# Routing a batch in parts and loading a later batch's input behind other transfers, in a Fourier mixing and mixture-of-experts kernel

## The chip, the cores and the metric

The kernel runs on one core of a Trainium2 chip. The core has a matrix engine (TensorE, PE in the profile, its weight loads PEld), a vector engine (VectorE, DVE), a scalar engine (ScalarE, ACT), GpSimd (POOL) and a queue engine (SyncE, SP), and 16 DMA engines that move data between the main memory and the on-chip memory. Each engine runs its own instructions in the order in which they were recorded, and waits on semaphores for the others. The metric is the time of one execution on the device, in microseconds (us).

## The reference

Two blocks follow each other. The first takes x of 8 batches, 2496 positions and 256 channels, and keeps the real part of a Fourier transform over both axes:

```python
X = np.fft.fft(x, axis=1)
X = np.fft.fft(X, axis=2)
return X.real.astype(np.float32)
```

The second treats the 19968 rows of the result as tokens of a mixture of 8 experts in which no token is dropped. Each token goes to the expert with the largest logit, through a hidden layer of 1024, and its result is scaled by that expert's probability:

```python
logits = x @ w_gate
expert_idx = np.argmax(logits, axis=1)
...
    h = np.maximum(x_sorted[lo:hi] @ w1[e], 0.0)
    y_sorted[lo:hi] = h @ w2[e]
return (gate_w[:, None] * y).astype(np.float32)
```

## The kernel before

The transform over 2496 positions is split as 104 times 24, and works batch by batch.

The first stage (`first`, line 325) reads x in three tiles per batch. `load` (284) issues one such transfer of 896 KB on SyncE's queue into one of three buffers `xq`. `fold` (299) adds and subtracts mirrored halves on VectorE, in two steps; `half1` (311) multiplies by the table of waves on TensorE (results `s1`), ScalarE copies them to `t1`, and a transfer writes them to a scratch tensor `Td` in main memory. `regroup` (351) reads `Td` back in another order as two tiles `t4`.

The second stage (`second`, 361) works in groups of 120 columns. `group` makes `p2` on TensorE, which ScalarE copies to `zz`; `turn_last` (365) is a small rotation `pr` of a column. Ten pairs of 128-row slices follow, five to each half: two products make `p3`, ScalarE copies part of it to `zs` (405), VectorE copies the logits to `lg` (408) and writes two slices of `rows` (410), and `mirror` (383), on ScalarE, fills the mirrored columns of the pair before.

`route` (416) then handles the five pairs of a half, ten slices, at once. VectorE finds the largest logit and its expert, one-hot in `oh`; TensorE counts the tokens ahead of each one with ten small products into `rk`; VectorE turns the counts into places `pi` in a buffer `Xs` in main memory that is sorted by expert. Each slice of `rows` is one scatter by index on GpSimd's queue (`send`, 462, through `put_row`, 235). A batch has 20 of them. For batches after 0, ScalarE and GpSimd first copy the index (468, 469).

`plan` (478) computes on one partition of VectorE which expert each block of rows belongs to. All its tables are 21 (`MOST`) columns wide, whatever the number of blocks. `experts` (729) works through the blocks: it fetches a block's rows `xb` (526) and the expert's weights (542) on SyncE's queue, transposes the rows (`turn`, 577: VectorE at 583, ScalarE at 586), and multiplies by the two weight matrices (`ph`, then `py`); another scatter on GpSimd writes the output. Batch 0 gives two blocks of 256 and four of 128 rows, batch 1 four of 256, the later ones blocks of 512.

The order of the work is that in which the Python program records it. Stages are generators, and each `yield` is a place at which other work can be woven in. Before any expert block: the first stage of batch 0; seven steps of `ahead_of(1)` (first stage and regrouping of batch 1); then `second(0)` with one more step of it at every second yield and a `send` at each. From line 996 on, `experts` drives the record: for every piece of expert work it does, side steps fall due (`next(side)`), and these are the plans, the next batches' stages and the sends. `mixed(b)` (935) weaves the second stage of batch b with the first stage of b + 1. The first block is recorded so, in lines 777 to 786:

```python
while todo[0][:3] not in tabs:
    yield 0, False
fetch_some(0, 1)
while b not in whole:
    yield 0, True
fetch_some(0)
for _ in range(9):
    yield 0, False
for xT in turn(b, size, xbs[0][0]):
    pass
```

Here each `yield 0, False` makes one side step, `fetch_some(0, n)` issues the row and weight fetches of the first n blocks, and `whole` holds a batch once all its scatters are recorded. Batch 2's three x tiles are loaded from within the first stage of batch 1 (line 344).

Of the kernel before, what the change touches and what calls it, by code (L numbers as in the profile page):

```python
# [12 lines left out]
F32 = mybir.dt.float32  # L13
BF16 = mybir.dt.bfloat16
# [167 lines left out]

TICKS = 32
LATE = 4
SHARE, EARLY, ROOM = 0.6, 0.7, 1.2
AHEAD = 12
WARM = 16
# [28 lines left out]
def kernel(ctx: ExitStack, tc, x, w_gate, w1, w2, out):  # L216
# [108 lines left out]
    def first(b):  # L325

        pm0 = xp.tile([NA, D], F32, tag="pm0", name="pm0")
        for q in range(NQ + 1):
            f = iter(())
            if q < NQ:  # L330
                xq = ahead.pop((b, q))
                f = fold(xq, q, pm0[:])
            next(f, None)
            yield
            if q:
                t1 = xp.tile([NP, 4, D], F32, tag="t1", name="t1")
                half1(b, q - 1, 0, pm, pm0, t1)
            next(f, None)
            yield
            if q:  # L340
                half1(b, q - 1, 1, pm, pm0, t1)
                (nc.sync if b > 1 else act).dma_start(out=Td[b][:, 4 * (q - 1) * D:4 * q * D], in_=t1[:].rearrange("p j d -> p (j d)"))
                if b:
                    load(b + 1, q - 1)
            next(f, None)
            pm = xq[:, 4:8]
            yield
# [13 lines left out]
    def second(b):  # L361

        t4 = None

        def turn_last(h):

            nonlocal t4
            t4 = ahead.pop((b, "t4", h))
            n = min(HALF, NG - h * HALF)
            pr = pm_.tile([GP, HALF], F32, tag="m", name="pr")  # L370
            mm(pr[:, 0:n], con["rot"][:], t4[0:GP, 0:n, H])
            act.copy(t4[0:GP, 0:n, H], pr[:, 0:n])

        def group(g):
            i, n = g % HALF, LAST if g == NG - 1 else GP
            p2 = pm_.tile([128, 2, n], F32, tag="m", name="p2")
            for c in range(2):
                mm(p2[:, c], t4[0:GP, i, c * H:(c + 1) * H], con["m2"][:, c, 0:n])
            act.copy(zz[:, :, g * GP:g * GP + n], p2[:])
            if g == HALF - 1:  # L380
                turn_last(1)

        def mirror(rows, k):
            act.copy(free(rows[:], (k + 1) * W + D - 1, [-W, 2], [-1, H - 1]),
                     free(rows[:], k * W + 1, [W, 2], [1, H - 1]))

        turn_last(0)
        yield
        group(0)
        yield  # L390
        group(1)
        yield
        for h in range(2):
            rows = sp.tile([128, NSL, W], F32, tag="rows", name="rows")
            lg = sp.tile([128, NSL, E], F32, tag="lg", name="lg")
            for i in range(HW):
                w, k = HW * h + i, 2 * i
# [18 lines left out]
    def route(b, h, rows, lg):  # L416
# [6 lines left out]
        mx, eq, v = small("mx", NSL), small("eq", NSL, E), small("v", NSL)  # L423
        vec.reduce_max(mx[:], lg[:], axis=AX_X)
        vec.tensor_tensor(eq[:], lg[:], bc(mx[:], 2, E), op=ALU.is_equal)
        vec.tensor_tensor(eq[:], eq[:], bc(con["rev"][:], 1, NSL), op=ALU.mult)
        vec.reduce_max(v[:], eq[:], axis=AX_X)
        vec.tensor_tensor(v[:], v[:], con["good"][:, h], op=ALU.mult)
        oh = small("oh", NSL + 1, E, dt=BF16)
        vec.memset(oh[:, NSL], 0.0)  # L430
        vec.tensor_tensor(oh[:, 0:NSL], bc(con["rev"][:], 1, NSL), bc(v[:], 2, E), op=ALU.is_equal)
        yield

        su = small("su", NSL)
        vec.tensor_tensor(lg[:], lg[:], bc(mx[:], 2, E), op=ALU.subtract)
        act.activation(lg[:], lg[:], ACTF.Exp)
        vec.tensor_scalar(rows[:, :, D], con["row"][:, h], float(b * S), None, op0=ALU.add)
        yield

        rk = pm_.tile([128, NSL + 1, E], F32, tag="m", name="rk")  # L440
        mm(rk[:], tri[:], oh[:], True, False)
        for s in range(NSL):
            mm(rk[:, s + 1:], ones[:], bc(oh[:, s], 1, NSL - s), False, s == NSL - 1)
        vec.reduce_sum(su[:], lg[:], axis=AX_X)
        vec.tensor_scalar(su[:], su[:], 1e-9, None, op0=ALU.add)
        vec.reciprocal(rows[:, :, D + 1], su[:])
        yield

        pos, pf, pi = small("pos", NSL, E), small("pf", NSL), small("pi", NSL, dt=I32)
        vec.tensor_tensor(pos[:], rk[:, 0:NSL], bc(base[:], 1, NSL), op=ALU.add)  # L450
        vec.tensor_tensor(pos[:], pos[:], oh[:, 0:NSL], op=ALU.mult)
        vec.reduce_sum(pf[:], pos[:], axis=AX_X)
        vec.tensor_tensor(pf[:] if b else pi[:], pf[:], con["far"][:, h], op=ALU.add)
        nxt = cp.tile([128, E], F32, tag="base", name="base", bufs=2)
        vec.tensor_tensor(nxt[:], rk[:, NSL], base[:], op=ALU.add)
        base = nxt
        for s in range(NSL):
            waiting.append((b, pf[:, s:s + 1], pi[:, s:s + 1], rows[:, s]))

    waiting = deque()  # L460
# [17 lines left out]
    def plan(b, size, k, last):  # L478
# [3 lines left out]
        def one(name, *dims, dt=F32):  # L482
# [14 lines left out]
        ge, ei = one("ge", MOST, E), one("ei", MOST)  # L497
        val, eq, rw = one("val", MOST, E + 1), one("eq", MOST, E + 1), one("rw", MOST)
        vec.tensor_tensor(ge[:], bc(bk["i"], 2, E), bc(ce[:], 1, MOST), op=ALU.is_ge)
        vec.reduce_sum(ei[:], ge[:], axis=AX_X)  # L500
        yield
        vec.tensor_tensor(eq[:], bc(ei[:], 2, E + 1), bc(bk["e9"], 1, MOST), op=ALU.is_equal)
        vec.memset(val[:, :, E:E + 1], float(E * CAP))
        vec.scalar_tensor_tensor(val[:, :, 0:E], bc(bk["i"], 2, E), float(size), bc(rb[:], 1, MOST),
                                 op0=ALU.mult, op1=ALU.add)
        yield
        vec.tensor_tensor(val[:], val[:], eq[:], op=ALU.mult)
        vec.reduce_sum(rw[:], val[:], axis=AX_X)
        tab = cp.tile([1, 2, MOST], I32, tag="p_tab", name="p_tab", bufs=4)
        vec.tensor_copy(tab[:, 0], rw[:])  # L510
        vec.tensor_scalar(tab[:, 1], ei[:], E - 1.0, None, op0=ALU.min)
# [217 lines left out]
    def experts(todo):  # L729
# [44 lines left out]
        for k, (b, size, last, at) in enumerate(todo):  # L774
            n, m = size // 128, BIG // size
            if not k:
# [303 lines left out]
```

## Time and profile before

| What | us |
|---|---|
| median of three runs | 1263.31 |
| lowest, highest | 1263.24, 1265.31 |
| the profiled execution's own time | 1264.13 |
| its span, from first to last instruction | 1262.3 |
| TensorE busy | 1214.1 |
| VectorE busy | 777.0 |
| ScalarE busy | 424.8 |
| GpSimd busy | 446.1 |

The page of a profile gives for each engine its busy time, its share of the span and its number of instructions; then the span in 40 equal slices, one digit of busy tenths each; then the chain of work that ended last, and the costliest groups by line, operation and tile. TensorE is busy for 96% of the span; its busy time is modelled for pipelined products, so it is read here for where it has gaps and not as a distance from the peak. Questions put to the trace answer for a stretch of time: busy times by stage, the chain of waits, the instructions in order, and how long a transfer took from its issue to its landing.

### The profile page before, as it was taken

What the parts mean: (1) busy time and instruction counts of PE and PEld (TensorE: products, weight loads), DVE (VectorE), ACT (ScalarE), POOL (GpSimd) and SP (SyncE); (2) the same over time, 40 slices, a digit from 0 to 9 for tenths busy, and PEclk for the clock granted to TensorE, in tenths of its full rate; (3) what the DMA queues carried; (4) which work ended last, traced back from release to release, by engine and by line L of the source; (5) the groups of instructions that cost most, each with busy time, mean ns of one, the idle gap of its engine ahead of it and who ended that gap; (6) DMA issues with size and microseconds to landing.
All of it is one profiled execution on the core that took longest, in us unless ns stands there. A gap on an engine that the chain in (4) does not pass through costs nothing.

```text
span 1262.3 us, 22196 instructions
## 1 busy us (share of the span) xinstructions
PE 1214.1 (96%) x7289; PEld 1080.3 (86%) x7289; DVE 777.0 (62%) x1884; ACT 424.8 (34%) x1087; POOL 446.1 (35%) x527
## 2 busy tenths in 40 slices
PE   5769999999999999999999999999999999999997
PEld 3658988777788899888988898889999999999996
DVE  4546334443466788576866578686888784444663
ACT  1423332332243433433344333432333232222222
POOL 0245436154116512472225603472364241111112
PEclk6759999999999999999999999999999999999998
DMA  8869898765348454573336435453346338788887
GB/s 236 272 195 327 304 307 306 204 224 169 126 147 258 138 142 160 154 263 115 101 123 207 141 94 160 140 179 101 105 138 190 109 105 282 284 289 275 285 284 278
DMA packets 163216, 249.79 MB, mean 198 GB/s; under 512 B 118601, under 2 KB 130227, under 8 KB 143516
## 3 DMA queue, kind: packets, MB, share of 16 engines
q1 hardware_dynamic: 146327, 203.28, 51.0%
q0 software_dynamic: 15888, 42.14, 9.3%
q10 hardware_dynamic: 885, 2.94, 0.7%
q8 instruction: 59, 0.97, 0.3%
q14 instruction: 57, 0.47, 0.1%
HBM read 194.91 MB, written 54.83 MB: 198 GB/s over the span
## 4 chain that ended last, share of the span: by engine, by line
PE 62%; issue 17%; DVE 10%; DMA 5%; POOL 4%; ACT 2%; POOLq 0%; SPq 0%; DVEq 0%; ACTq 0%
PE py L221 18%; PE a L221 9%; PE c L221 7%; PE ph L221 6%; PE p L221 6%; PE b L221 5%; PE d L221 4%; PE s L221 3%; PE e L221 3%; POOL out_dram L236 3%; DMA t<-Td 1%; DMA xq<-in_x_dram 1%; POOL Xs L236 1%; DVE xT L583 1%; DMA Td<-t 1%
## 5 line engine op out<-in xcount | busy, mean ns | idle before, releaser
L236 POOL DMA_INDIRECT out_dram<-y,ro x163 | 160.9, 987 | 629.5 <-ACT y L679 299.6
L221 PE MATMUL py<-w_sb,hT 128*128 128x256 f32 x1504 | 340.3, 380 | 0.0
L221 PEld LDWEIGHTS py<-w_sb,hT 128*128 128x128 f32 x1504 | 281.2, 190 | 36.9 <-issue 1.0
L236 POOL DMA_INDIRECT Xs<-rows,pi x160 | 164.2, 1026 | 111.7 <-DVE rows L410 53.0
L221 PE MATMUL ph<-xT,w_sb 128*128 128x128 f32 (+2 forms) x992 | 173.1, 330 | 10.0 <-DVE ro L792 8.8
L221 PEld LDWEIGHTS ph<-xT,w_sb 128*128 128x128 f32 x992 | 137.6, 194 | 34.4 <-issue 16.5
L221 PE MATMUL a<-xT,w_sb 128*128 128x256 f32 (+1 forms) x512 | 117.9, 357 | 0.0
L837 DVE TENSOR_SCALAR hT<-ph 128x512 f32<-128x512 f32 x43 | 29.7, 691 | 127.9 <-PE ph L221 68.2
L586 ACT ACTIVATE xT<-xT 128x256 f32<-128x256 f32 (+1 forms) x94 | 36.5, 388 | 181.7 <-DVE xT L583 137.3
L221 PEld LDWEIGHTS a<-xT,w_sb 128*128 128x128 f32 x512 | 88.5, 190 | 10.0 <-DVE xT L583 0.3
L891 ACT ACTIVATE y<-py,xb 128x256 f32<-128x256 f32 x94 | 44.5, 473 | 153.8 <-PE py L221 152.1
L635 DVE TENSOR_TENSOR hT<-hT,b 128x512 f32<-128x512 f32 x57 | 39.2, 687 | 79.0 <-PE b L221 53.4
L408 DVE COPY lg<-p 128x16 f32<-128x16 f32 x80 | 13.8, 173 | 111.4 <-ACT zs L405 111.3
L645 ACT ACTIVATE hT<-a 128x512 f32<-128x512 f32 x57 | 34.0, 597 | 134.1 <-PE a L221 131.1
L221 PE MATMUL s<-xq,w 104*112 104x256 f32 (+2 forms) x208 | 62.4, 425 | 11.8 <-DVE xq L297 9.5
L469 POOL CAST pi<-due 128x1 int32<-128x1 f32 x140 | 42.2, 302 | 68.4 <-ACT due L468 68.4
L221 PE MATMUL a<-w_sb,hT 128*128 128x128 f32 x528 | 66.0, 276 | 0.0
L221 PEld LDWEIGHTS p<-table,t 120*128 120x128 f32 x352 | 54.7, 206 | 10.6 <-issue 3.1
L221 PEld LDWEIGHTS a<-w_sb,hT 128*128 128x128 f32 x528 | 63.1, 192 | 0.7
L221 PE MATMUL c<-xT,ws 128*128 128x256 f32 (+1 forms) x256 | 60.2, 362 | 1.2 <-DVE hT L641 0.4
L221 PE MATMUL p<-table,zz 128*128 128x145 f32 (+1 forms) x320 | 57.6, 306 | 3.6 <-DVE rows L410 2.4
L583 DVE STREAM_TRANSPOSE xT<-xb 128x512 f32<-128x512 f32 (+1 forms) x91 | 56.3, 631 | 7.0 <-DMA xb<-Xs 7.0
(149 smaller groups left out, 2103.2 us busy)
## 6 DMA issues: line engine op xcount, KB each, us to landing
w_sb<-in_moe_w_dram SPq DMA_DIRECT2D x132, 1024.0 KB, 6.9
xq<-in_x_dram SPq DMA_DIRECT2D x24, 896.0 KB, 8.9
xb<-Xs SPq DMA_DIRECT2D x112, 128.0 KB, 3.3
Td<-t SPq DMA_DIRECT2D x18, 448.0 KB, 3.3
t<-Td SPq DMA_DIRECT2D x8, 768.0 KB, 7.0
t<-Td SPq DMA_DIRECT2D x8, 640.0 KB, 9.3
xb<-Xs SPq DMA_DIRECT2D x52, 64.0 KB, 4.7
xb<-Xs SPq DMA_DIRECT2D x88, 32.0 KB, 4.8
```

The lines of the kernel that those rows point to most:

```text
L221: nc.tensor.matmul(o, lhsT=lhsT, rhs=rhs, start=start, stop=stop, **kw)
L236: return unordered(pool.indirect_dma_start(out=dst, out_offset=bass.IndirectOffsetOnAxis(ap=idx, axis=0), in_=rows, in_offset=None, bounds ...
L408: vec.tensor_copy(lg[:, k:k + 2], p3[:, NY:NY + 2 * E].rearrange("p (m e) -> p m e", m=2))
L469: pool.tensor_copy(idx, due[:])
L583: vec.transpose(free(xT[:], 256 * h, [32, n // 32], [BIG, 2], [1, 32]), free(xb, 512 * h, [64, n // 32], [1, 2], [2, 32]))
L586: act.activation(odd, odd, ACTF.Copy, scale=-1.0)
L635: vec.tensor_tensor(h12, h11, b[:], op=add)
L645: act.activation(h11, a[:], ACTF.Relu)
L837: vec.tensor_scalar(o, ph[:], 0.0, None, op0=ALU.max)
L891: act.activation(y[:, i % 2], py[:], ACTF.Copy, scale=meta[:, i, 1:2])
```

## The change

Six things are changed.

- Batch 0 is routed in four parts, of 2, 3, 3 and 2 pairs (`PARTS`), each with its own counts and scatters. The first two steps of a part's route are recorded at once and the rest after the rows of the next pair.
- VectorE's copy of the logits becomes a ScalarE copy, recorded after the mirror.
- The x tiles of batch 2 are no longer loaded from the first stage of batch 1. The first is loaded after batch 1's regrouping; the second and third are loaded in `experts`, after the fetches of the first two blocks and before the third's.
- Before `second(0)` six steps of batch 1's first stage are recorded and not seven; inside it, one step at each yield from the seventh on, in place of every second.
- In `mixed` the first stage's steps fall on even steps of the second stage in place of odd. Before the first transposition stand 12 side steps in place of 9, and the first five steps of the plans come before the weaving.
- `plan` works on k columns, the number of blocks, in place of `MOST`.

```diff
+PARTS = ((2, 3), (3, 2))
@@ first
-                if b:
+                if b > 1:
                     load(b + 1, q - 1)
@@ second
+            ends = list(np.cumsum(PARTS[h] if not b else (HW,)))
+            lo = 0
...
-                if i:
+                if i and i not in ends:
                     mirror(rows, k - 2)
-                vec.tensor_copy(lg[:, k:k + 2], p3[:, NY:NY + 2 * E].rearrange("p (m e) -> p m e", m=2))
+                act.copy(lg[:, k:k + 2], p3[:, NY:NY + 2 * E].rearrange("p (m e) -> p m e", m=2))
...
+                if pending:
+                    for _ in pending:
+                        pass
+                    pending = None
                 yield
-            mirror(rows, k)
-            yield from route(b, h, rows, lg)
+                if i + 1 in ends:
+                    mirror(rows, k)
+                    pending = route(b, h, rows, lg, slice(lo, k + 2))
+                    if not b and w < NW - 1:
+                        next(pending)
+                        next(pending)
+                    else:
+                        yield from pending
+                        pending = None
+                    lo = k + 2
@@ route: the same operations on n slices, with pf and pi in four buffers
+        n = at.stop - at.start
+        rows, lg = rows[:, at], lg[:, at]
...
@@ plan: the same operations on k columns
-        vec.tensor_tensor(ge[:], bc(bk["i"], 2, E), bc(ce[:], 1, MOST), op=ALU.is_ge)
+        vec.tensor_tensor(ge[:, :, 0:E], bc(count, 2, E), bc(ce[:], 1, k), op=ALU.is_ge)
...
@@ experts
                 while b not in whole:
                     yield 0, True
+                fetch_some(0, 2)
+                load(2, 1)
+                load(2, 2)
                 fetch_some(0)
-                for _ in range(9):
+                for _ in range(12):
                     yield 0, False
@@ ahead_of
         regroup(b, 0)
         regroup(b, 1)
+        if b == 1:
+            load(2, 0)
@@ mixed
-            if k % 2:
+            if k % 2 == 0:
                 next(one, None)
@@ before the expert blocks
-    for _ in range(7):
+    for _ in range(6):
         next(early)
     for k, _ in enumerate(second(0)):
-        if k % 2 == 0:
+        if k >= 6:
             next(early, None)
         send()
...
-            side = woven(chain(close(0), through(0)), chain(early, side))
+            plans = close(0)
+            side = chain(islice(plans, 5), woven(chain(plans, through(0)), chain(early, side)))
```

More of the change, by code (lines that the diff above doesn't have):

```diff
@@ L411, in second, with route @@
                                              op0=ALU.add, op1=op)
+                if pending:
+                    for _ in pending:
+                        pass
+                    pending = None
                 yield
-            mirror(rows, k)
-            yield from route(b, h, rows, lg)
-    def route(b, h, rows, lg):
+                if i + 1 in ends:
[6 more added lines that the diff above has]
+                        yield from pending
+                        pending = None
+                    lo = k + 2
+    def route(b, h, rows, lg, at):
         nonlocal base
@@ L421, in small @@
             return sp.tile([128, *dims], dt, tag=name, name=name)
[L423 to L429, printed above, removed]
@@ L430, in route @@
-        vec.memset(oh[:, NSL], 0.0)
-        vec.tensor_tensor(oh[:, 0:NSL], bc(con["rev"][:], 1, NSL), bc(v[:], 2, E), op=ALU.is_equal)
+        n = at.stop - at.start
+        rows, lg = rows[:, at], lg[:, at]
+        mx, v, su = (small(name, NSL)[:, 0:n] for name in ("mx", "v", "su"))
+        eq, pos = (small(name, NSL, E)[:, 0:n] for name in ("eq", "pos"))
+        pf = sp.tile([128, NSL], F32, tag="pf", name="pf", bufs=4)[:, 0:n]
+        pi = sp.tile([128, NSL], I32, tag="pi", name="pi", bufs=4)[:, 0:n]
@@ L432, in route @@
+        oh = small("oh", NSL + 1, E, dt=BF16)[:, 0:n + 1]
+        vec.reduce_max(mx, lg, axis=AX_X)
+        vec.tensor_tensor(eq, lg, bc(mx, 2, E), op=ALU.is_equal)
+        vec.tensor_tensor(eq, eq, bc(con["rev"][:], 1, n), op=ALU.mult)
+        vec.reduce_max(v, eq, axis=AX_X)
+        vec.tensor_tensor(v, v, con["good"][:, h, at], op=ALU.mult)
+        vec.memset(oh[:, n], 0.0)
+        vec.tensor_tensor(oh[:, 0:n], bc(con["rev"][:], 1, n), bc(v, 2, E), op=ALU.is_equal)
         yield
-        su = small("su", NSL)
@@ L435, in route @@
-        vec.tensor_tensor(lg[:], lg[:], bc(mx[:], 2, E), op=ALU.subtract)
-        act.activation(lg[:], lg[:], ACTF.Exp)
-        vec.tensor_scalar(rows[:, :, D], con["row"][:, h], float(b * S), None, op0=ALU.add)
+        vec.tensor_tensor(lg, lg, bc(mx, 2, E), op=ALU.subtract)
+        act.activation(lg, lg, ACTF.Exp)
+        vec.tensor_scalar(rows[:, :, D], con["row"][:, h, at], float(b * S), None, op0=ALU.add)
         yield
-        rk = pm_.tile([128, NSL + 1, E], F32, tag="m", name="rk")
@@ L441, in route @@
[L441 to L446, printed above, removed]
-        yield
-        pos, pf, pi = small("pos", NSL, E), small("pf", NSL), small("pi", NSL, dt=I32)
-        vec.tensor_tensor(pos[:], rk[:, 0:NSL], bc(base[:], 1, NSL), op=ALU.add)
@@ L451, in route @@
-        vec.tensor_tensor(pos[:], pos[:], oh[:, 0:NSL], op=ALU.mult)
-        vec.reduce_sum(pf[:], pos[:], axis=AX_X)
-        vec.tensor_tensor(pf[:] if b else pi[:], pf[:], con["far"][:, h], op=ALU.add)
+        rk = pm_.tile([128, NSL + 1, E], F32, tag="m", name="rk")[:, 0:n + 1]
+        mm(rk, tri[:], oh, True, False)
+        for s in range(n):
+            mm(rk[:, s + 1:], ones[:], bc(oh[:, s], 1, n - s), False, s == n - 1)
+        vec.reduce_sum(su, lg, axis=AX_X)
+        vec.tensor_scalar(su, su, 1e-9, None, op0=ALU.add)
@@ L454, in route @@
+        vec.reciprocal(rows[:, :, D + 1], su)
+        yield
+        vec.tensor_tensor(pos, rk[:, 0:n], bc(base[:], 1, n), op=ALU.add)
+        vec.tensor_tensor(pos, pos, oh[:, 0:n], op=ALU.mult)
+        vec.reduce_sum(pf, pos, axis=AX_X)
+        vec.tensor_tensor(pf if b else pi, pf, con["far"][:, h, at], op=ALU.add)
         nxt = cp.tile([128, E], F32, tag="base", name="base", bufs=2)
-        vec.tensor_tensor(nxt[:], rk[:, NSL], base[:], op=ALU.add)
+        vec.tensor_tensor(nxt[:], rk[:, n], base[:], op=ALU.add)
@@ L456, in route @@
         base = nxt
-        for s in range(NSL):
+        for s in range(n):
             waiting.append((b, pf[:, s:s + 1], pi[:, s:s + 1], rows[:, s]))
@@ L496, in plan @@
         vec.scalar_tensor_tensor(rb[:], ex[:], -float(size), gone[:], op0=ALU.mult, op1=ALU.add)
-        ge, ei = one("ge", MOST, E), one("ei", MOST)
-        val, eq, rw = one("val", MOST, E + 1), one("eq", MOST, E + 1), one("rw", MOST)
-        vec.tensor_tensor(ge[:], bc(bk["i"], 2, E), bc(ce[:], 1, MOST), op=ALU.is_ge)
-        vec.reduce_sum(ei[:], ge[:], axis=AX_X)
+        ge, val, eq = (one(name, MOST, E + 1)[:, 0:k] for name in ("ge", "val", "eq"))
+        ei, rw = (one(name, MOST)[:, 0:k] for name in ("ei", "rw"))
+        count = bk["i"][:, 0:k]
+        vec.tensor_tensor(ge[:, :, 0:E], bc(count, 2, E), bc(ce[:], 1, k), op=ALU.is_ge)
+        vec.reduce_sum(ei, ge[:, :, 0:E], axis=AX_X)
         yield
-        vec.tensor_tensor(eq[:], bc(ei[:], 2, E + 1), bc(bk["e9"], 1, MOST), op=ALU.is_equal)
+        vec.tensor_tensor(eq, bc(ei, 2, E + 1), bc(bk["e9"], 1, k), op=ALU.is_equal)
         vec.memset(val[:, :, E:E + 1], float(E * CAP))
-        vec.scalar_tensor_tensor(val[:, :, 0:E], bc(bk["i"], 2, E), float(size), bc(rb[:], 1, MOST),
+        vec.scalar_tensor_tensor(val[:, :, 0:E], bc(count, 2, E), float(size), bc(rb[:], 1, k),
                                  op0=ALU.mult, op1=ALU.add)
         yield
-        vec.tensor_tensor(val[:], val[:], eq[:], op=ALU.mult)
-        vec.reduce_sum(rw[:], val[:], axis=AX_X)
+        vec.tensor_tensor(val, val, eq, op=ALU.mult)
+        vec.reduce_sum(rw, val, axis=AX_X)
         tab = cp.tile([1, 2, MOST], I32, tag="p_tab", name="p_tab", bufs=4)
-        vec.tensor_copy(tab[:, 0], rw[:])
-        vec.tensor_scalar(tab[:, 1], ei[:], E - 1.0, None, op0=ALU.min)
+        vec.tensor_copy(tab[:, 0, 0:k], rw)
+        vec.tensor_scalar(tab[:, 1, 0:k], ei, E - 1.0, None, op0=ALU.min)
         if last:
```

## The prediction

> **What bounds the kernel now.** I read the page first, for where TensorE is not full; then busy time by stage; then the chain of waits over the bad stage; then SyncE's own queue and the x transfers' landings.
>
> ```profile
> PE 1214.1 (96%) x7289; PEld 1080.3 (86%) x7289; DVE 777.0 (62%) x1884; ACT 424.8 (34%) x1087; POOL 446.1 (35%) x527
> ...
> PE   5769999999999999999999999999999999999997
> ```
>
> One digit is 31.6 us. TensorE is full from slice 4 on; between 140 and 1200 us its busy times by stage leave 5.6 us idle. So only the first 90 us are left to win, and any delay of the first expert block shows in the end undiminished.
>
> ```profile
> 70.00:80.00 10.00, 5.91 (x21) 4.39 (x19) 6.99 (x29) 2.91 (x10) 8.00 (x7) 0.62 0.79 296
> 80.00:87.00 7.00, 0.00 (x0) 0.00 (x0) 0.39 (x1) 0.00 (x0) 0.97 (x1) 0.50 0.32 70
> 87.00:95.00 8.00, 7.63 (x27) 6.61 (x28) 2.00 (x9) 2.35 (x6) 0.00 (x0) 0.63 0.71 215
> ```
>
> Columns: stage, length, busy time of PE, weight loads, DVE, ACT, POOL, granted clock, DMA share, GB/s. From 80 to 87 TensorE does nothing. The chain of waits says why:
>
> ```profile
> 78.86 0.97 POOL Xs L236
> 79.83 0.30 issue
> 80.14 2.41 DMA Xs<-rows,pi
> 82.79 0.35 SPq L535
> 83.34 0.34 SPq L535
> 83.89 0.32 SPq L535
> 84.40 2.09 DMA xb<-Xs
> 86.61 0.71 DVE xT L583
> 87.38 3.77 PE ph L221 x8
> ```
>
> GpSimd's 20 scatters of batch 0 (starts 53.47 to 80.14, 1.40 us apart on average, 1.28 undisturbed) end last. Their landing at 82.55 lets SyncE fetch block 0 (82.79); it is transposed at 86.61, and the first expert product starts at 87.37.
>
> What SyncE issues next matters as much (start, issue time, tile, count):
>
> ```profile
> 82.79 1.92 SPq L535 DMA_DIRECT2D xb<-Xs  x4
> 84.91 0.40 SPq L539 DMA_DIRECT2D xb<-Xs  x1
> 86.09 2.29 SPq L535 DMA_DIRECT2D xb<-Xs  x4
> 88.59 0.40 SPq L539 DMA_DIRECT2D xb<-Xs  x1
> 89.78 0.37 SPq L545 DMA_DIRECT2D w_sb<-in_moe_w_dram  x1
> 90.33 0.34 SPq L547 DMA_DIRECT2D w_sb<-in_moe_w_dram  x1
> 90.78 0.37 SPq L342 DMA_DIRECT2D Td<-t  x1
> 91.25 0.58 SPq L289 DMA_DIRECT2D xq<-in_x_dram  x1
> ```
>
> Rows of block 0, rows of block 1, block 1's weights (2 MB), then a write and an x load: 8.5 us from first to last. The tile of x between 25 and 115 us adds how long such a load takes:
>
> ```profile
> DMA to landing us min/median/max: 8.4/10.2/11.9
> ```
>
> **The change part by part.**
>
> *Half 1 moved back* (six steps of batch 1's first stage ahead of the second stage, not seven). In before, batch 0's regrouped rows land at 34.64 and the first rows come out at 42.74; two pairs of s products stand between (35.06 to 36.88, 38.58 to 40.28: 3.5 us). Without them the first rows come at 39.7 (bounds 39.2 to 42.7).
>
> *Four routes in place of two.* One route holds VectorE from 48.98 to 52.53: 3.55 us for ten rows. Its operations take 0.17 us on 10 elements and 0.24 on 80, so with 4 or 6 rows a route is 2.8 to 3.4; I take 3.0. Four are 12.4 in place of 7.1. The counting products become 24 small ones for 22: nothing. Each part is followed on VectorE by the next pair's rows (0.6). Walking VectorE: pair 1's rows end at 42.2; part 1's indices, after a route, a pair and 0.7 of waiting, at 46.5. Part 2: two pairs 1.2, the fold of x that stood earlier 2.75 (39.91 to 42.65), a pair 0.6, a route 3.0, waits 1.3: 55.4. Part 3: 1.2, 0.6, 3.0, waits 2.6: 62.8. Part 4: 0.6, 3.1, the Exp wait 0.3: 66.8.
>
> GpSimd began 0.93 after its indices (52.54 to 53.47). At 1.40 us a send: part 1's four run 47.4 to 53.0; it idles to 56.3; six to 64.7; six to 73.1; the last of four starts at 77.3 and lands 2.41 later, at 79.7. At 1.28 it is 77.9. So batch 0 is whole at 78.8, not 82.55: 3.8 us won (bounds 0 and 4.7). Six to seven us of earlier start shrink to that because VectorE cannot deliver part 2 in time. SyncE's first fetch of rows moves to 79.0.
>
> *Batch 2's x loaded later.* This is the term that decides. In before its three loads are issued at 33.3 to 49.6. In the built order of after, the first stands behind batch 1's regrouping. The second and third stand in SyncE's queue behind the row fetches of blocks 0 and 1 and block 1's weights: all that follows the last scatter above, but for the write. Yet VectorE's order has the fold of the second x tile, and with it the wait for that load, ahead of the transposition of block 0, since the twelve side steps come between. Issue: 79.0 + 8.46 - 0.47 = 87.0. Landing: 8.4 to 11.9 us later; the top row had weights and a write ahead of it, this one the weights, so I take the median, 10.2: 97.2. Then, in the order of each queue: fold 2.5 (26.88 to 29.40), pair 0's rows 0.6, TensorE's cold group and pair (0.9 and 1.2, as at 36.88 and 65.37) with ScalarE's mirror, copy of logits and t copy between them 1.1, ScalarE's zs, mirror and logits 0.7, the rows 0.6, and transposition to product 0.8 (86.61 to 87.37): 8.4 with every step exposed, 6.4 with the copies hidden; I take 7.4. First expert product at 104.6, not 87.37: +17.2. Bounds: 77.9 + 0.2 + 8.0 + 8.4 + 6.4 = 100.9 (+13.5), and 82.8 + 8.5 + 11.9 + 8.4 = 111.6 (+24.2).
>
> What else waits there: TensorE is queued behind the same rows (its next group needs the pair's PSUM), so it has nothing to run. SyncE stops at the write of batch 2's first tile, whose copy now ends about 4 us after the landing; block 2's rows and weights (2 MB, 6.9 us by the page) are then there by about 118, and in before that block began 46 us after the first product: covered.
>
> Here the Trainium skill, "DMA: Bandwidth & Descriptors", section Bandwidth, can be set against the row: it measured 341 GB/s for a transfer of 1 MB, and more for larger ones, which speaks for a shorter wait. By that figure the 2 MB of weights and 0.9 MB of x would take an estimated 8.8 us from the weights' issue, land at 94.8, and make the sum 2.4 us less. No run here shows such a pair alone, so the row stands.
>
> *Left undone at the first product.* Before 87.37 the old order had one more group, rotation and pair done: 0.44 + 0.13 + 0.51 at full clock (starts at 140.35 to 141.94), +1.1.
>
> *Side steps on even ticks.* Batch 3's regrouping moves ahead of one block's row and weight fetch on SyncE. In before it is issued at 199.72 and TensorE waits 2.32 us for it at 211.60; about 7 us earlier the wait goes: -2.3 (bounds -2.3, 0). Next due there is the ScalarE copy behind it.
>
> *Logits by ScalarE.* 80 copies of 0.17 us leave VectorE; ScalarE's nearest are 0.17 to 0.20. VectorE's rows now wait for the signal behind the mirror and the copy, 0.6 us later a pair, in the 70 pairs beside expert blocks. VectorE already waits 111 us for zs there while TensorE idles 5.6 of 1060: cover is ample. 0, bounds -2 and +2; were the cover gone, 70 x 0.57 = 40.
>
> *Plans on k columns.* 21 columns cost 0.31 to 0.34 us, 8 wide 0.15 to 0.17; some 0.9 us a plan, off the path but for a 1.15 us wait of TensorE at 121.28 behind VectorE: -0.5 (0, -1.2).
>
> Sum against the profiled execution (1264.13 around a span of 1262.3): 17.2 + 1.1 - 2.3 - 0.5 = +15.5, so 1279.6. That execution lies 0.8 above the median 1263.31: 1278.8.
>
> **The rivals.** *The routing gain alone (faster).* If the second x tile were in before the transposition, the first product would follow the scatters as now: 79.0 + 4.6 = 83.6, -3.8, with +1.1, -2.3 and -0.5: 1257.8. For it: the gap at 80 to 87 is real and this is what shrinks. It decides only if the landing plus 7.4 is before 86.3 (87.37 less the 1.1 left undone), so the landing before 79; but the load is issued no sooner than 8 us after the scatters. Against it stands the order of two queues. 0.06.
>
> *The scatters end no earlier.* If VectorE and ScalarE hand each other the pairs more slowly (rows now wait for the logits' copy), part 4 or GpSimd ends as late as before, 82.55: all of the above 3.8 later, 1282.6. For it: ScalarE held the rows up 13.3 us before 100 us. 0.22.
>
> *The loads land fast.* With 8.4 and 6.4 in place of 10.2 and 7.4: 1276. 0.15. *The stages behind also suffer* from the mirror's wait: up to +2 and a stall kept, 1283. 0.05.
>
> **How the numbers follow.** The forecast has 0.50, with 1275 to 1284 of its own; the slower rivals 0.42; faster 0.06; 0.02 for cancelling. Low: 1263.3 + 13.5 + 1.1 - 2.3 - 1.2 - 2 = 1272.4, put at 1271 for what is not in the sum. High: 1263.3 + 24.2 + 1.1 = 1288.6, cut to 1288. 0.2% (2.5 us) is about what a measurement can tell.
>
> **What would show it.** Right: GpSimd's first scatter near 47, the last landing near 79; the second load of batch 2 issued near 87; a VectorE wait of ten us or more for x before the first transposition; first ph near 105; no wait at batch 3's rotation. Wrong: no such wait, or a first ph before 90; or idle time returning after 140.

## The result, and the profile after

| | median us | lowest to highest | ratio to before, 95% interval |
|---|---|---|---|
| before | 1264.31 (4 runs) | 1263.24 to 1265.37 | |
| after | 1282.09 (4 runs) | 1282.02 to 1283.82 | 1.0149, 1.0134 to 1.0164 |

The changed kernel is 17.8 us slower. The forecast's sum gave 1278.8, with a range of 1271 to 1288. The profiled execution took 1282.03 us around a span of 1280.3.

The page of the changed kernel, its busy times and its slices:

```profile
PE 1213.5 (95%) x7291; PEld 1081.1 (84%) x7291; DVE 764.6 (60%) x1838; ACT 431.7 (34%) x1169; POOL 443.8 (35%) x527
...
PE   5726999999999999999999999999999999999997
```

TensorE has the same work (1213.5 us against 1214.1). Its fourth slice, 96 to 128 us, was full and is now at 6; the third, 64 to 96, falls from 6 to 2. Between 64 and 128 us it is busy for 29.7 us in place of 51.2, and the end of the span moves by 18.0.

Busy time by stage (columns as before: stage, length, PE, weight loads, DVE, ACT, POOL, granted clock, DMA share, GB/s):

```profile
70.00:80.00 10.00, 2.46 (x10) 2.18 (x10) 5.17 (x22) 0.89 (x3) 5.07 (x6) 0.50 1.04 389
80.00:87.00 7.00, 6.35 (x24) 5.42 (x24) 1.05 (x9) 1.92 (x6) 0.00 (x0) 0.62 0.57 185
87.00:95.00 8.00, 0.00 (x0) 0.00 (x0) 0.00 (x0) 0.00 (x0) 0.00 (x0) 0.61 0.67 203
95.00:105.00 10.00, 0.08 (x1) 0.08 (x1) 3.10 (x6) 0.10 (x1) 0.00 (x0) 0.50 0.86 259
105.00:113.00 8.00, 5.95 (x19) 4.88 (x19) 1.89 (x6) 2.30 (x9) 0.00 (x0) 0.52 0.72 195
```

Two things are to be seen. From 87 to 104.9 TensorE has nothing: the hole ahead of the first expert product, 8.8 us long before (78.55 to 87.37), has become one of 18.3. And from 70 to 80 the DMA engines are full (share 1.04, 389 GB/s), where before they moved 296.

The chain of waits over that stretch (start, length, what):

```profile
75.62 6.96 DMA Xs<-rows,pi
82.84 0.35 SPq L555
...
91.18 10.53 DMA xq<-in_x_dram
101.73 1.24 DVE xq L307
...
108.64 0.63 DVE xT L603
109.31 2.93 PE ph L222 x6
```

GpSimd's last scatter goes out at 75.62, 4.5 us earlier than before (80.14), but takes 6.96 us to land instead of 2.41. SyncE starts on block 0 at 82.84 (before: 82.79). Then the chain leaves the rows and runs through the x load, as forecast. SyncE's queue shows why it starts at 91.18 (start, issue time, tile, count):

```profile
82.84 2.28 SPq L555 DMA_DIRECT2D xb<-Xs  x4
85.31 0.40 SPq L559 DMA_DIRECT2D xb<-Xs  x1
86.49 1.87 SPq L555 DMA_DIRECT2D xb<-Xs  x4
88.95 0.40 SPq L559 DMA_DIRECT2D xb<-Xs  x1
90.18 0.36 SPq L565 DMA_DIRECT2D w_sb<-in_moe_w_dram  x1
90.73 0.35 SPq L567 DMA_DIRECT2D w_sb<-in_moe_w_dram  x1
91.18 0.99 SPq L290 DMA_DIRECT2D xq<-in_x_dram  x2
```

TensorE's waits from 100 us to the end (total, times, longest):

```profile
PE p L222 <- DVE rows L414: 18.3, 1, 18.3
PE ph L222 <- DVE xT L603: 2.1, 1, 2.1
PE p L222 <- ACT t L373: 2.0, 4, 0.8
PE ph L222 <- DVE hT L860: 1.2, 1, 1.2
```

The 18.3 us are the wait for a pair's rows, which stand behind the fold of the late x on VectorE. The wait of 2.32 us for batch 3's regrouping, at 211.60 before, is gone.

### The profile page after: what moved, and what is told of

It reads as the page before. It is cut to its first block, busy times and chain, and to the rows that moved or that the text cites. A ratio compares the mean times of both kernels' runs of the same rounds, so it can differ in the third digit from the quotient of the medians.

```text
span 1280.3 us, 22332 instructions
## 1 busy us (share of the span) xinstructions
PE 1213.5 (95%) x7291; PEld 1081.1 (84%) x7291; DVE 764.6 (60%) x1838; ACT 431.7 (34%) x1169; POOL 443.8 (35%) x527
## 4 chain that ended last, share of the span: by engine, by line
PE 82%; DVE 9%; DMA 4%; ACT 2%; issue 2%; SPq 0%; POOL 0%; POOLq 0%; DVEq 0%; ACTq 0%
PE py L222 24%; PE ph L222 12%; PE a L222 11%; PE c L222 9%; PE p L222 6%; PE b L222 6%; PE d L222 5%; PE e L222 4%; PE s L222 3%; DMA xq<-in_x_dram 1%; DVE xT L603 1%; DMA Td<-t 1%; DVE y L703 1%; DMA t<-Td 1%; DMA Xs<-rows,pi 1%
## 5 line engine op out<-in xcount | busy, mean ns | idle before, releaser
L237 POOL DMA_INDIRECT Xs<-rows,pi x160 | 159.0, 994 | 107.7 <-DVE base L474 46.5
L222 PEld LDWEIGHTS ph<-xT,w_sb 128*128 128x128 f32 x992 | 136.5, 192 | 27.6 <-issue 16.8
L414 DVE SCALAR_TENSOR_TENSOR rows<-p,zs 128x129 f32<-128x129 f32 x160 | 48.9, 348 | 138.4 <-ACT lg L412 136.5
L860 DVE TENSOR_SCALAR hT<-ph 128x512 f32<-128x512 f32 x43 | 29.7, 691 | 122.1 <-PE ph L222 62.1
L222 PE MATMUL p<-table,t 120*128 120x120 f32 (+1 forms) x352 | 59.0, 295 | 20.7 <-DVE rows L414 18.3
L488 POOL CAST pi<-due 128x1 int32<-128x1 f32 x140 | 45.3, 323 | 93.3 <-ACT due L487 93.2
L222 PEld LDWEIGHTS s<-xq,w 104*112 104x112 f32 x208 | 37.9, 202 | 29.7 <-DVE xq L298 17.0
```

The lines of the kernel that those rows point to most:

```text
L222: nc.tensor.matmul(o, lhsT=lhsT, rhs=rhs, start=start, stop=stop, **kw)
L237: return unordered(pool.indirect_dma_start(out=dst, out_offset=bass.IndirectOffsetOnAxis(ap=idx, axis=0), in_=rows, in_offset=None, bounds ...
L488: pool.tensor_copy(idx, due[:])
L860: vec.tensor_scalar(o, ph[:], 0.0, None, op0=ALU.max)
```

## The experiments

`e1` to `e4` ran on a chip on which the kernel before took 1271.25 us (1266.84 to 1274.57, 20 runs), and are compared with that; the others stood beside 1264.22 and 1262.89 of the kernel before.

**The load move, from both sides.** First the old kernel with nothing but batch 2's loads at their new places (`e3_load_move_alone`):

```diff
-                if b:
+                if b > 1:
                     load(b + 1, q - 1)
@@ ahead_of
+        if b == 1:
+            load(2, 0)
@@ experts
+                fetch_some(0, 2)
+                load(2, 1)
+                load(2, 2)
                 fetch_some(0)
```

> The kernel before, with the move of batch 2's three x loads as its only edit. Theory A: the scatters land at 82.6 as before, the second x tile is issued near 91 and lands near 102, and VectorE's fold of it holds up the rows and the first transposition: first expert product at 107 to 112, time 1284 to 1289 (1264.3 and 20 to 25). Rival C: the move alone costs less than 4 us, 1268 or less.

1295.27 us against 1271.25: 24.0 slower, ratio 1.0198 (1.0167 to 1.0229), as theory A had it. The two loads go out together and the first expert product follows them (SyncE's queue, then TensorE's instructions):

```profile
90.88 1.06 SPq L289 DMA_DIRECT2D xq<-in_x_dram  x2
```

```profile
104.64 1.34 PE L221 MATMUL p<-table,zz 128*128 128x145 f32 x4 [20.76 <-DVE rows L410]
112.24 3.72 PE L221 MATMUL ph<-xT,w_sb 128*128 128x256 f32 x8 [1.76 <-DVE ro L795]
```

Then the opposite: the changed kernel with these three lines back at their old places, all else changed. `e2_old_loads`, `e7_old_loads_again` and `e9_old_loads_third` are this one kernel; `e6_after_again` is the changed kernel itself, beside it.

> The changed kernel, with the x tiles of batch 2 loaded from the first stage of batch 1 as in the kernel before; all else as changed. Theory A: no wait of VectorE for x before the first transposition. Theory B: with 0.9 MB less behind the regrouping the last scatter lands 2.4 to 5 us after its issue at about 75.6, so at 78 to 81; the first expert product starts 4.7 us later, at 83 to 86, and the time is 1256 to 1259, faster than before. Rival C: 1275 or more. A middle one, that the queue is the same with the weights alone: the scatters land at 82.6, the first product at 87.3, the time 1260.

> The changed kernel itself, so that the runs of its parts stand beside it on one chip. Theory (the x loads cost the time): 1.0149 of the time before, as first measured, within 0.003, on whatever chip; the second x load of batch 2 is issued about 91 us and lands some 10 us later, the first block's first product stands at 109. Rival (the time lost depends on the chip's other stalls, since the runs of the parts showed idle time at 62 to 72 us that the first profile of the changed kernel has not): the ratio is nearer 1.008, as without the twelve side steps.

> The changed kernel with batch 2's x loads at their old place, once more beside the changed kernel itself. Theory: the load move is all of the loss, so this stands 15 to 22 us below the changed kernel and within 0.2% of the one before or up to 0.4% under it (the last scatter can land 1 to 4 us earlier, because 0.9 MB less waits in the queues at 66 to 82 us). Rival (twelve steps, plan and logits cost something by themselves): over 0.2% above the kernel before.

> The changed kernel with batch 2's x loads at their old place, in more rounds, as the base of the two runs beside it. Theory (the rest of the change is a small gain, mostly the stall of TensorE for batch 3's regrouping that is gone): 0.9975 to 0.999 of the time before. Rival (the rest of the change is worth nothing): 0.9995 to 1.0005.

| | median us | before us | ratio |
|---|---|---|---|
| `e2_old_loads` | 1271.01 | 1271.25 | 1.0010 (0.9993 to 1.0028) |
| `e6_after_again` | 1282.39 | 1264.22 | 1.0146 (1.0120 to 1.0171) |
| `e7_old_loads_again` | 1261.76 | 1264.22 | 0.9985 (0.9971 to 1.0000) |
| `e9_old_loads_third` | 1262.33 | 1262.89 | 0.9993 (0.9979 to 1.0008) |

On one chip, the loads' place is worth 1282.39 - 1261.76 = 20.6 us. That is more than the whole loss; by the medians of the three runs all the other edits together are worth between -0.2 and -2.5 us (intervals of the ratio from 0.9971 to 1.0028). The repeat of the changed kernel agrees with the first (1.0149). The gain that theory B of `e2` hoped for (1256 to 1259) did not come. For `e9` neither its theory (0.9975 to 0.999) nor its rival (0.9995 to 1.0005) is ruled out.

**Where in the queue the loads stand.** The loads behind the regrouping, but ahead of the row fetches (`e1_loads_before_fetch`):

```diff
         if b == 1:
             load(2, 0)
+            load(2, 1)
+            load(2, 2)
@@ experts
-                fetch_some(0, 2)
-                load(2, 1)
-                load(2, 2)
```

> The changed kernel, with the second and third x tile of batch 2 loaded right behind the first one, so ahead of the row fetches and weights of the first blocks in SyncE's queue. Theory A (VectorE's wait for the second x tile, 20.5 us ahead of the first transposition, is the loss): the tiles are there before the scatters land, the first expert product starts at 88 to 91 in place of 109.3 and the time is 1282.1 - 20 = 1262, within 3 us. With it goes theory B, that the scatters land late because other transfers are queued (6.96 us for the last one): 1.8 MB more stand ahead of them, so the last scatter lands at 84 to 88 and not at 82.6. Rival C (the four routes, the ScalarE copies or the new weave make the loss): the time stays at 1275 or more.

1278.60 against 1271.25, ratio 1.0053 (1.0034 to 1.0072): about a third of the changed kernel's loss (1.0149) is left. The loads go out at 73.03, and the first product comes at 96.91. Theory A missed: it had the first product at 88 to 91 and the time of the kernel before. Theory B's landing, 84 to 88, came (85.6). Now the 2.7 MB compete with the scatters and the rows: the second block's row fetch takes 5.79 us to issue, where it takes 1.87 in the changed kernel. Earlier in the same crowded stretch is better, but not free: on the same chip, `e2` with the old places is 7.6 us faster. Its last scatter also goes out 2.9 us later than in the changed kernel (78.55), behind a stall of that chip that the last section shows; how much of the loss is due to that was not separated.

**The order on VectorE.** The changed kernel without the twelve side steps ahead of the first transposition, so that VectorE transposes block 0 before it folds the late x. `e4` and `e12` are this one kernel:

```diff
-                for _ in range(12):
-                    yield 0, False
```

> The changed kernel without the twelve side steps between the fetches and the first transposition; the x tiles are loaded where the change loads them. Theory A, in the form that it is the order on VectorE and TensorE and not the late load itself that costs: the first transposition no longer stands behind the fold, the first expert product starts at 86.5 to 88, block 0 has about 18 us of work on TensorE that needs no x, and the fold's wait ends at 102 beside it; the time is 1260 to 1266. If the late load itself costs (whatever waits for it stops the rest): the first product is early, but TensorE stops later for 10 us or more, 1272 to 1280.

> The changed kernel without the twelve side steps ahead of the first transposition, beside runs on the same chip. VectorE then transposes block 0's rows before it folds the late x. Theory A (the loss is the order on VectorE alone: the transposition stands behind the wait for x): the first product comes at about 90 and the end falls back to within 4 us of the kernel before. Theory B (TensorE has no other work until x is there, so the lateness of x costs it wherever it stands): the first product is early but TensorE stops later for about as long, and the ratio stays at 1.006 to 1.012, some half of the loss.

1281.81 against 1271.25 (ratio 1.0084, 1.0054 to 1.0113), and 1272.17 against 1262.89 (1.0070, 1.0049 to 1.0092). So about half of the loss goes. TensorE's instructions of the second run:

```profile
88.79 9.86 PE L222 MATMUL ph<-xT,w_sb 128*128 128x256 f32 x32 [21.98 <-DVE ro L813]
...
106.45 0.70 PE L222 MATMUL p<-table,t 120*128 120x120 f32 x4 [2.38 <-ACT zz L380]
```

The first product stands at 88.79, 20 us earlier than in the changed kernel, and the later stop for x is only 2.38 us. Theory A, a time within 4 us of the kernel before, missed. Theory B had the size right and the reason wrong: TensorE does not stop later for about as long. What is paid instead is the wait in front, 21.98 us. The same execution by stage, beside the kernel before:

```profile
60.00:84.00 24.00, 3.19 (x30) 2.52 (x29) 10.25 (x63) 2.54 (x11) 12.57 (x13) 0.64 0.82 273
```

```profile
60.00:84.00 24.00, 13.61 (x52) 11.49 (x52) 16.14 (x67) 5.54 (x17) 16.83 (x15) 0.57 0.65 228
```

Before, TensorE is busy for 13.61 us in this stretch, mostly with batch 1's work; without the steps for 3.19. The 10.4 us that it misses are left for later, where TensorE is full; the loss is 9.3. So with the late load either order costs: with the steps ahead, the first block is held up; without them, the hole ahead of the block stays empty. The kernel with the old loads and without the steps was not run, so how much of the empty hole is due to the late x, and how much to leaving out the steps, stays open.

**What the four routes are worth.** The kernel with the old loads and two parts of five pairs:

```diff
-PARTS = ((2, 3), (3, 2))
+PARTS = ((5,), (5,))
```

> As the run with the loads at their old place, but batch 0 routed in two parts of five pairs instead of four. It prices the four parts. Theory A, by the issue of the scatters: the last scatter goes out some 4 us later (79 to 80 us against 75.6 in the changed kernel) and the end is 3 to 4 us later than with four parts. Theory B, by what is queued on the DMA engines: the last scatter lands within 1.5 us of where it lands with four parts, and the end moves by less than 1.5 us.

1262.95 us, ratio 0.9986 (0.9974 to 0.9998), beside 0.9985 with four parts: four parts are worth nothing. The first scatter goes out 4.3 us later (50.29 against 45.98), the last one only 0.8 us (77.11 against 76.35). The chain with two parts:

```profile
77.11 5.00 DMA Xs<-rows,pi
82.11 0.02 SPq L555
```

SyncE's first fetch is at 82.36 with two parts and at 83.08 with four. Theory B's numbers hold, but the condition of theory A, a last issue at 79 to 80, did not come about, so this run alone does not decide between them. The runs that do not have the stall of the last section, side by side, say more:

| run | last scatter issued | SyncE's first row fetch |
|---|---|---|
| before | 80.14 | 82.79 |
| after | 75.62 | 82.84 |
| `e6_after_again` | 73.92 | 81.47 |
| `e7`, old loads, four parts | 76.35 | 83.08 |
| `e9`, the same | 74.58 | 82.08 |
| `e8`, old loads, two parts | 77.11 | 82.36 |
| `e10`, old loads, odd steps (below) | 74.00 | 81.25 |
| `e11`, last load behind (below) | 76.69 | 84.57 |
| `e12`, no steps | 75.83 | 84.13 |
| `e5`, late weights (below) | 74.26 | 79.64 |

The kernel before issues its last scatter latest of all, and yet all others but `e5` fetch within 1.8 us of it, on either side. Among the kernels with four parts and early weights the fetch comes 6.7 to 8.3 us after the issue, and 2.65 before: most of what they gain in the issue is lost in the landing. Only `e5`, with less on the DMA engines, fetches clearly sooner.

**What holds up the landing.** The changed kernel with block 0's 2 MB of weights fetched behind the scatters:

```diff
-                fetch_some(0, 1)
                 while b not in whole:
                     yield 0, True
```

> The changed kernel with block 0's weights (2 MB) fetched behind the scatters' landing instead of before it. Theory B (the last scatter lands 6.96 us after its issue because 4.3 MB of regrouping, x and weights are queued ahead of it): 2.3 MB are left ahead of it, so it lands 2.4 to 3.6 us after its issue, at 78 to 79.5, and SyncE's first row fetch starts at 78.5 to 80 instead of 82.84. Rival (the scatter itself, or the pace of the pairs, is slow): the landing stays within 1 us of 82.6. The weights then stand ahead of the x load in the queue, so the first product of block 0 comes between 104 and 111 either way, and the end between 1276 and 1284.

The chain of waits, and busy time by stage at its end:

```profile
74.26 5.14 DMA Xs<-rows,pi
79.39 0.02 SPq L555
```

```profile
76.50:77.00 0.50, 0.00 (x0) 0.00 (x0) 0.00 (x0) 0.00 (x0) 0.00 (x0) 0.50 0.99 339
77.00:77.50 0.50, 0.00 (x0) 0.00 (x0) 0.00 (x0) 0.00 (x0) 0.00 (x0) 0.50 0.47 149
77.50:78.00 0.50, 0.00 (x0) 0.00 (x0) 0.05 (x1) 0.00 (x0) 0.00 (x0) 0.50 0.01 0
```

The changed kernel beside it (`e6`):

```profile
73.92 7.31 DMA Xs<-rows,pi
```

The landing comes after 5.14 us in place of 7.31, at 79.39 in place of 81.23. The rival falls: the scatter is held up by what else is on the DMA engines. But only part of it is the weights; the forecast of 2.4 to 3.6 us was too short. The regrouping and x that are still there keep the engines full until 76, and from 76.5 on nearly all of what moves, 0.24 MB, is of GpSimd's own queue: the scatters had fallen behind. The kernel is not faster, 1284.67 us (ratio 1.0158, 1.0125 to 1.0191), just above the 1276 to 1284 that were forecast: the weights are now ahead of the x load, and the first product is at 109.81.

**Batch 3's stage in the odd steps again**, on the kernel with the old loads:

```diff
-            if k % 2 == 0:
+            if k % 2:
                 next(one, None)
```

> The same, but batch 3's first stage drawn in the odd steps again, as before the change. It prices the term of 2.3 us for batch 3's earlier regrouping. Theory: TensorE waits about 2.3 us for that regrouping again (near 211 us in the kernel before, near 212 here) and the end is 2.0 to 2.5 us later than without this edit. Rival (the wait went for another reason, such as the plan or the weave of batch 0): no such wait, and the end within 0.7 us.

TensorE's instruction at batch 3's rotation:

```profile
210.57 0.37 PE L222 MATMUL pr<-t,table 120*120 120x6 f32 x2 [3.02 <-DMA t<-Td]
```

The wait is back, so the even steps are what removes it. The 2.0 to 2.5 us that were forecast can't be told in the time: 1262.84 us against 1262.33, ratios 1.0004 (0.9988 to 1.0020) and 0.9993 (0.9979 to 1.0008). In the two profiled executions the first expert product stands 2.0 us earlier with the odd steps (86.46 against 88.44) and the end 1.2 us later, so some 3 us are lost between.

**The last load behind the regrouping**, an attempt at a faster kernel:

```diff
-                if b:
+                if b > 1 or b and q < NQ:
                     load(b + 1, q - 1)
@@ ahead_of
+        if b == 1:
+            load(2, NQ - 1)
```

> Loads at their old place, but the last of batch 2's three x loads goes out behind batch 1's two regrouping transfers instead of ahead of them. Theory (with the load ahead, the store before the regrouping takes 7.4 us to land and the regrouping goes out at 70.8 us): the store lands in 3 to 4 us, the regrouping goes out at 66 to 67, TensorE's work on batch 1's first pairs starts 3 to 4 us sooner, the first block's first product stands at 86.5 to 87.5 instead of 89.05, and the end is 1 to 2.5 us earlier. Rival (what sets the first product is the scatters' landing behind the same bytes): the end moves by less than 0.7 us.

1262.15 us beside 1262.33: the rival, by its time. The first half of the theory came true. With the load ahead (`e9`), the store is issued at 61.58 and the regrouping can go out at 69.69, 8.1 us later; with it behind, 63.70 and 66.89, 3.2 us. TensorE's instructions with the load ahead, then behind:

```profile
76.31 0.57 PE L222 MATMUL pr<-t,table 120*120 120x6 f32 x2 [11.54 <-DMA t<-Td]
...
88.44 2.01 PE L222 MATMUL ph<-xT,w_sb 128*128 128x256 f32 x8 [2.38 <-DVE xT L603]
```

```profile
72.96 0.57 PE L222 MATMUL pr<-t,table 120*120 120x6 f32 x2 [6.08 <-DMA t<-Td]
...
88.94 3.78 PE L222 MATMUL ph<-xT,w_sb 128*128 128x256 f32 x8 [4.79 <-DVE xT L603]
```

TensorE's side work starts and ends earlier, but the first block still waits for the scatters, whose landing is no earlier (first row fetch 84.57, and 82.08 in `e9`). The longer pause ahead of it (4.79 us) leaves the clock low: eight products take 3.78 us, and 2.01 where the side work ended just before.

The lowest ratio of all these kernels is 0.9985: none is measurably better than the one before by more than a fraction of a per cent.

## Why the prediction was right, step by step

- **The mechanism is the one forecast.** The term that was to decide did: loads behind two blocks' rows and a block's weights in SyncE's queue, the fold ahead of the transposition in VectorE's. The chain above shows it, and both tests of the load's place confirm it. Against the same change with x there in time (1257.8), the forecast had 1278.8: 21.0 us. Measured, `e6` against `e7`: 20.6. The path agrees less closely than the time: the first product stands at 107.31 and 89.05 there, 18.3 us apart.
- **SyncE's queue.** From first row fetch to load 8.34 us, forecast 8.0. From the load's issue to the fold 10.55, forecast 10.2. From there to the first product 7.58, forecast 7.4. Together 0.9 over.
- **"So batch 0 is whole at 78.8, not 82.55: 3.8 us won."** This step failed. The parts were ready nearly on time (46.0, 55.6, 62.6, 67.3; forecast 46.5, 55.4, 62.8, 66.8), the first scatter went out at 46.97 (47.4) and the last at 75.62 (75.5 to 77.3). But its landing was taken as 2.41 us from a row in which the DMA engines were mostly idle; before, then in the changed kernel:

```profile
80.00:82.00 2.00, 0.00 (x0) 0.00 (x0) 0.00 (x0) 0.00 (x0) 0.97 (x1) 0.50 0.32 112
```

```profile
80.00:82.00 2.00, 1.77 (x4) 1.41 (x5) 1.05 (x9) 0.00 (x0) 0.00 (x0) 0.50 1.03 420
```

  In the changed kernel regrouping, x load and weights, 4.3 MB, go out between 65.98 and 71.92, and the engines run at 404 to 420 GB/s from 76 to 82. In the kernel before, the regrouping had gone out at 56.43 and only the weights later (68.75). So the regrouping, 9.5 us later in the new order of steps, is most likely in the way, and not the x load alone: with the old loads (`e7`, `e9`) it goes out at 70.81 and 69.69 and the fetch is within 0.8 us of that before (83.08, 82.08). No run moves the regrouping alone. The forecast never added up these bytes, and took the price of the last scatter alone, though others of the same batch took up to 6.7 us in the kernel before, as the view of the tile `Xs` from 40 to 84 us has it (its minimum is of a row fetch):

```profile
DMA to landing us min/median/max: 1.9/4.1/6.7
```

  Nothing of the 3.8 us is left: SyncE's first row fetch is at 82.84, before at 82.79.
- **The rival "the scatters end no earlier"** has the number of the result, 1282.6 against 1282.09, but not its reason: the parts were ready on time, so there was no slower hand-over between VectorE and ScalarE.
- **First product at 104.6.** It came at 109.31: 3.8 for the lost gain, 0.9 for the queue.
- **What was given back, and the luck in it.** A delay of the first block was to show in the end undiminished. But the first product is 21.9 us late and the end of the span 18.0: 3.9 us are made up behind it, where the forecast's terms had 1.7 (+1.1, -2.3, -0.5). So 2.2 us too much given back hide part of the first product's 4.7 us, and the sum is nearer than its terms. The term that was mis-sized is the wait for batch 3's regrouping. TensorE at batch 3's rotation, before and after:

```profile
211.60 0.37 PE L221 MATMUL pr<-t,table 120*120 120x6 f32 x2 [2.32 <-DMA t<-Td]
...
212.76 3.37 PE L221 MATMUL ph<-xT,w_sb 128*128 128x256 f32 x8
```

```profile
232.52 0.28 PE L222 MATMUL pr<-t,table 120*120 120x6 f32 x2
...
233.75 1.90 PE L222 MATMUL ph<-xT,w_sb 128*128 128x256 f32 x8
```

  The wait is gone, as forecast, but it had cost more than its 2.32 us: behind it the granted clock was 0.57 from 212 to 216, and the eight products took 3.37 us in place of 1.90. From the end of the 24 products ahead of the rotation to the end of these eight, the kernel before takes 6.85 us and the changed one 2.97. The forecast had 2.3 and no clock in it. "Left undone at the first product, +1.1" is there as work: 7053 products of TensorE stand from the first expert product on, 7043 before, and the ten are a group, a rotation and a pair. Up to the rotation the lag grows from 21.9 to 23.4 us; there it falls to 19.5, and to 18.0 at the end. These last 1.5 us are not traced.
- **Logits by ScalarE, 0:** nothing speaks against it. VectorE waits 136.5 us for that copy in all, and TensorE's idle time between 140 and 1200 us is 5.1 us and was 5.6. Without the wait at batch 3's rotation (2.3, before) and the wait in block 1 that falls into this window only in the changed kernel (1.2), 3.9 stand against 3.3. No run takes this edit alone.
- **Plans, -0.5:** wrong. The wait of TensorE in block 1 is still there, 1.23 us at 144.43 (1.15 at 121.28 before).
- **341 GB/s for 1 MB** ("DMA: Bandwidth & Descriptors", section Bandwidth) led to an estimate of 8.8 us from the weights' issue to the landing; it took 11.55 (90.18 to 101.73). In that time the DMA engines moved 3.47 MB at 301 GB/s: the rate was lower, and half a megabyte more went through than the estimate counted, because the third x tile goes out together with the second and shares the engines. The row of 10.2 us was nearer.
- **Its own signs.** The first scatter near 47, VectorE's wait for x (20.5 us) and the missing wait at batch 3's rotation came; the last landing near 79 and the load near 87 did not (82.6 and 91.18).

## What to carry to other kernels

Before you put a transfer later in a queue, read two orders, not one: what stands ahead of it there, and what stands behind its consumer on the consumer's engine. A stretch in which an engine idles is not a place to load into, if what ends the stretch is itself a transfer; add up the bytes of all queues in it before you take a landing time from a quieter row. And work that fills a wait is worth its time only as long as its own data are already there.

## What the runs showed of the hardware

- How long a scatter takes to land goes with how busy the DMA engines are from its issue to its landing: 2.41 us in the kernel before (share 0.27), 4.65 in `e3_load_move_alone` (0.51), 5.00 with two parts (0.63), 5.14 with the late weights (0.92 until 77.5, then next to nothing), and 6.48 to 8.05 in the changed kernel and six of its variants (0.97 to 1.07). In the changed kernel from 72 to 80 us, GpSimd's queue gets 26.9% of the 16 engines' time and SyncE's 76.6%.
- In the run with the late weights the DMA engines move next to nothing from 77.5 on, yet the scatter's landing is seen at 79.39, 1.9 us after. The Trainium skill puts about 2 us of fixed cost on a transfer, most of it the receipt for the last byte ("DMA: Bandwidth & Descriptors", section Anatomy of one DMA — SWDGE (gpsimd) path); the 1.9 us agree with it, though the trace does not show what fills them.
- A pause of TensorE can be paid twice, by the wait and by the clock after it. The first block's first eight products take 3.64 us in the changed kernel, where TensorE had done 2.3 us of work since a hole of 18.3 (granted clock of the stage 0.52), 3.78 in the run with the last load behind, after a pause of 4.79 (0.71), and 2.01 in `e9`, where side work had run from 76.31 until 2.4 us before them (1.00): 1.6 to 1.8 us for eight products. At batch 3's rotation in the kernel before, the low clock (0.57) follows a wait of 2.32 us; in `e9` it does not follow a wait of 2.38, so the length of the pause alone does not decide.
- On the chip of the first four runs the profiles have a stall that nothing in them explains. The waits of `e2_old_loads` from 58 to 76 us:

```profile
PE rk L222 <- issue: 8.2, 1, 8.2
POOL Xs L237 <- issue: 6.4, 10, 3.2
...
ACT t L322 <- remote: 6.0, 1, 6.0
```

ScalarE waits 6 us for products that TensorE had issued 5 us before, and the chain of `e1_loads_before_fetch` calls 6.37 us there "another core or an unknown queue". `e4_no_steps` has a wait of 5.7 us of this kind, and `e3_load_move_alone`, the old kernel with the load move, two of 3.5 and 3.9. The profiled execution of `e2` is also the slowest of its ten (1277.43, median 1271.01). The same programs run later (`e7`, `e12`) do not show the stall. It stays open. What rests on that chip alone is the run with the loads ahead of the row fetches and that with the load move in the old kernel.
